# Gelu in front of the main loop: fewer VectorE steps, constants on ScalarE, multiplies on GpSimd, four PSUM banks for the running maxima

## The chip, the cores and the metric

The kernel runs on one core of one Trainium2 chip. The core has a matrix engine (TensorE, PE in the profile; its weight loads are PEld), VectorE (DVE), ScalarE (ACT), GpSimd (POOL) and SyncE (SP), which here only issues transfers. Each engine takes its own instructions strictly in the order in which the program wrote them, and waits where an operand isn't ready. The metric is the device time of one execution in microseconds; the median of three runs before the change is 1665.98 us (1665.54 to 1667.02).

## The reference

Two branches work on the same 2048 x 640 input and are mixed by a gate per token:

```python
def _A_ref(x, wq, wk, wv, wo):                  # H = 32 heads of 20, one shared k and v
    scores = jnp.einsum("bhqd,bkd->bhqk", q, k) * (Dh ** -0.5)
    p = _softmax(scores, axis=-1)
    o = jnp.einsum("bhqk,bkd->bhqd", p, v)
    return o.transpose(0, 2, 1, 3).reshape(B, S, H * Dh) @ wo
def _B_ref(x, w1, b1, w2, b2):                  # mixes over tokens: S = 2048, F = 1728
    h = _layernorm(x, axis=-1)
    u = _gelu(jnp.einsum("bsd,sf->bdf", h, w1) + b1)        # tanh form of gelu
    y = jnp.einsum("bdf,fs->bds", u, w2) + b2
    return y.transpose(0, 2, 1)
g = _sigmoid((x * gate_w).sum(-1, keepdims=True))
return g * _A_ref(...) + (1 - g) * _B_ref(...)
```

## The kernel before

Products that need more than the matrix engine's reduced precision are split in a high and a low part: a tile is rounded to `wh` (high), and `wl = raw - wh` is the low part; a product is then three matrix products (high by high, high by low, low by high).

The program has three stretches. First come projections of q, k and v and the layer norm (0 to about 96 us). Then follows the stretch that the change touches, called the **front loop** here (lines 565 to 601, about 96 to 168 us). Last comes the **main loop** (from line 1079 on), which does scores, exponentials, the product with v, the rest of the token mixing, and the output.

**The front loop** computes the first PRO = 8 of the 14 blocks of 128 columns of `h @ w1` for one half of the channels. A block is 16 *steps* (one row tile of 128 tokens each); a step is three products, each cut into two halves of 64 rows that go to two banks of PSUM, `pu0` and `pu1` (six matrix instructions a step, line 586). Four steps use one *chunk* of weights `wr`, `wh`, `wl`, so a block has four chunks, called hf 0 to hf 3. Ahead of each chunk `w1_upto` (line 118) prepares the chunk that is used three chunks later: the high part by ACT (line 126) for chunks below 4 * PRO = 32 and by POOL (line 128) from there on, the low part by POOL always (line 129), and it has SP fetch the raw weights of a further chunk (line 101). There are four buffers each of `wr`, `wh` and `wl`, so a chunk's high part can't be written before PE is through with the chunk four places earlier.

Between the steps stand 48 *leads* (`lead`, line 569): each issues two matrix instructions for the row maxima of the attention scores (line 479, tile `ms`) and two VectorE reductions that read them from PSUM (line 482, tile `mp`). They are spread from step 3 to step 122 of the 128. Before the change `ms` rotates through three banks, the pool `ps_m`; the pool `ps_g`, one bank, lies unused until the main loop; `pu0` and `pu1` have two banks each on the other side of PSUM.

After the last step of a block `gelu` (line 515) writes one ACT instruction, bias added while reading `pu0` (line 519; `id` in the text), and hangs the rest on the list `chain`. After each step of the next block `pop_chain` takes one entry, `None` for nothing. So entry *i* stands in each engine's queue behind step *i* of the next block, and `w1_upto` for hf 1, 2 and 3 stands in front of steps 4, 8 and 12. Before the change the entries are

```python
chain.extend((None, None, add, None, cube, tanh, None, prod_p, None, None, None, high, None, low))
```

| entry | what it writes | engine, line |
|---|---|---|
| 2 `add` | add the half in `pu1`; then square | DVE 525; ACT 522 |
| 4 `cube` | (square + constant) times x | DVE 529 |
| 5 `tanh` | tanh | ACT 532 |
| 7 `prod_p` | plus one; times x | POOL 545, 546 |
| 11 `high` | high part of the result | ACT 535 |
| 13 `low` | low part | POOL 538 |

For the last of the eight blocks `add` and the square are written at once, and the rest comes in the main loop by another list (`cube_p`, `tanh`, `prod_p`, `high_p`), where `settle` pops it. Between the two loops line 1016 prepares one more chunk.

**The main loop** puts its score and maximum products alternately into the banks of `ps_m` and `ps_s` (three each, `next_bank`, line 459), and token mixing products into `ps_g`. `ps_s` and `ps_o` open at lines 603 and 604 over the banks that `pu0` and `pu1` leave. The order of all queues is the program's own (`tc.manual_schedule`, line 170).

Of the kernel before, what the change touches and what calls it, by code (L numbers as in the profile page):

```python
# [9 lines left out]
F32 = mybir.dt.float32  # L10
F32R = mybir.dt.float32r
AF = mybir.ActivationFunctionType
ALU = mybir.AluOpType
AX = mybir.AxisListType
PSUM = bass.MemoryType.PSUM
DRAM = bass.MemoryType.DRAM

P = 128
# [6 lines left out]
NB = 512  # L25
# [3 lines left out]
PRO = 8  # L29
# [10 lines left out]
def mix_kernel(ctx: ExitStack, tc: tile.TileContext, A_x, A_wq, A_wk, A_wv, A_wo,  # L40
               B_x, B_w1, B_b1, B_w2, B_b2, gate_w, out):
    nc = tc.nc
# [3 lines left out]
    def f32(ap):  # L46
        return ap.bitcast(F32)
# [10 lines left out]
    bias = const.tile([P, 32], F32, name="bias")  # L58
# [19 lines left out]
    right = ExitStack()  # L78
# [13 lines left out]
    def w1_load(n):  # L92
        while len(w1raw) < min(n, len(chunks)):
            c = len(w1raw)
            wr = w1r.tile([P, HS, P], F32, name="wr")
            if c < W2:
                fc, hf = chunks[c]
                rows = slice(hf * HS * P, (hf + 1) * HS * P)
                for o in range(0, P, P if fc < FC - 1 else FT):
                    fw = P if fc < FC - 1 else FT  # L100
                    nc.sync.dma_start(out=wr[:, :, o:o + fw],
                                      in_=B_w1[rows, fc * P:fc * P + fw].rearrange("(c p) f -> p c f", p=P))
            else:
                st, hf = chunks[c]
                cols = slice(st * P, (st + 1) * P)
                nf = min(HS, FC - 1 - hf * HS)
                if hf == 3:
                    for h in range(2):
                        nc.sync.dma_start(out=wr[64 * (1 - h):64 * (2 - h), 2:, :],
                                          in_=B_w2[:2 * P, cols].rearrange("(c h p) s -> h p c s", c=2, h=2)[h])  # L110
                nc.sync.dma_start(out=wr[:, :nf, :],
                                  in_=B_w2[hf * HS * P:(hf * HS + nf) * P, cols].rearrange("(c p) s -> p c s", p=P))
                if nf < HS:
                    for o in range(0, P, FT):
                        nc.sync.dma_start(out=wr[o:o + FT, nf, :], in_=B_w2[(FC - 1) * P:, cols])
            w1raw[c] = wr

    def w1_upto(n):
        while fetched[0] < min(n, len(chunks)):
            c = fetched[0]  # L120
            w1_load(c + 1)
            wr = w1raw[c]
            wh = w1p.tile([P, HS, P], F32R, name="wh")
            wl = w1p.tile([P, HS, P], F32R, name="wl")
            if c < 4 * PRO:
                nc.scalar.activation(wh, wr, AF.Copy)
            else:
                nc.gpsimd.tensor_copy(wh, wr)  # L128
            nc.gpsimd.tensor_sub(wl, wr, f32(wh))  # L129
            w1t[c] = wh, wl  # L130
            fetched[0] += 1
            w1_load(c + 4)
# [22 lines left out]
    def new_q(n):  # L155
        if n < NU:
            qtiles[n] = load_q(n, "qst")
# [289 lines left out]
    u_lo = [view(t, UC * HD2, UC) for t in (u0, slot[0])]  # L447
    pp_pool = ctx.enter_context(tc.tile_pool(name="pp", bufs=11))
    ev = ctx.enter_context(tc.tile_pool(name="ev", bufs=1))
    ps_m = ctx.enter_context(tc.tile_pool(name="ps_m", bufs=3, space=PSUM))  # L450
    ps_g = ctx.enter_context(tc.tile_pool(name="ps_g", bufs=1, space=PSUM))
    mpool = ctx.enter_context(tc.tile_pool(name="mpool", bufs=2))
    mmpool = ctx.enter_context(tc.tile_pool(name="mmpool", bufs=2))

# [3 lines left out]

    def next_bank():
        if not ring:  # L460
            return ps_m.tile([P, NB], F32, name="ms")
        ring[0] ^= 1
        return ps_m.tile([P, NB], F32, name="ms") if ring[0] else ps_s.tile([P, NB], F32, name="s")
    given = [0, 0]
# [2 lines left out]
    def ms_next(b):  # L467
        k = given[b]
        if k >= 32 * NU:
            return None  # L470
        given[b] += 1
        n, r = divmod(k, 32)
        (kq, pr), qt = divmod(r // 4, 2), r % 4

        def step():
            if n not in mtiles:
                mtiles[n] = mpool.tile([P, 16, 4], F32, name="mp")
            ms = next_bank()
            nc.tensor.matmul(ms, qmax[n][64 * b:64 * b + 60, pr, qt * P:(qt + 1) * P],  # L479
                             kst[64 * b:64 * b + 60, kq * NB:(kq + 1) * NB], start=True, stop=True)  # L480
            c = (2 * b + pr) * 4 + qt
            nc.vector.tensor_reduce(mtiles[n][:, c, kq:kq + 1], ms, axis=AX.X, op=ALU.max)  # L482
            issued[b] += 1
            if min(issued) == 32 * n + 1:
                new_qmax(n + 1)

        return step
# [25 lines left out]
    chain = []  # L513

    def gelu(d, fc, accs):
        both = fin.tile([P, D], F32, name="yo")
        xg, t1 = both[:, :HD2], both[:, HD2:]
        hi, lo = u_hi[d][:, fc, :], u_lo[d][:, fc, :]
        nc.scalar.activation(xg, accs[0][:, :HD2], AF.Identity, bias=bias[:, NS + fc:NS + fc + 1])

        def square():
            nc.scalar.activation(t1, xg, AF.Square)

        def add():
            nc.vector.tensor_add(xg, xg, accs[1][:, :HD2])  # L525
            square()

        def cube():
            nc.vector.scalar_tensor_tensor(t1, t1, 1.0 / 0.044715, xg, op0=ALU.add, op1=ALU.mult)

        def tanh():
            nc.scalar.activation(t1, t1, AF.Tanh, scale=GC * 0.044715)

        def high():
            nc.scalar.activation(hi, t1, AF.Copy)

        def low():
            nc.gpsimd.tensor_sub(lo, t1, f32(hi))

        def cube_p():  # L540
            nc.gpsimd.tensor_scalar(t1, t1, 1.0, 1.0 / 0.044715, op0=ALU.mult, op1=ALU.add)
            nc.gpsimd.tensor_mul(t1, t1, xg)

        def prod_p():
            nc.gpsimd.tensor_scalar(t1, t1, 1.0, 1.0, op0=ALU.mult, op1=ALU.add)
            nc.gpsimd.tensor_mul(t1, t1, xg)

        def high_p():
            nc.gpsimd.tensor_copy(hi, t1)
            nc.gpsimd.tensor_sub(lo, t1, f32(hi))  # L550

        if len(accs) == 2 and fc == PRO - 1:
            add()
            chain.extend((cube_p, None, tanh, prod_p, high_p))
        elif len(accs) == 2:
            chain.extend((None, None, add, None, cube, tanh, None, prod_p, None, None, None, high, None, low))
        else:
            chain.extend((square, cube_p, None, tanh, prod_p, high_p))

# [2 lines left out]
        if f:  # L562
            f()

    with tc.tile_pool(name="psb", bufs=2, space=PSUM, side="right") as psb:
        at, skip, last = 0, 3, NS * PRO - 6
        one_by_one[0] = True

        def lead():
            for b in range(2):  # L570
                ms_next(b)()
            ms_done()

        for fc in range(PRO):
            pu = [psb.tile([P, NB], F32, name=f"pu{r}") for r in range(2)]
            for hf in range(4):
                w1_upto(4 * fc + hf + 4)
                for f in [q_parts_due.pop(0) for _ in range(min(len(q_parts_due), 1 + fc // 5))] if fc else []:
                    f()
                wh, wl = w1t.pop(4 * fc + hf)  # L580
                for c in range(HS):
                    st = hf * HS + c
                    for k, (w, h) in enumerate(((wh, h_hi[0]), (wh, h_lo[0]), (wl, h_hi[0]))):
                        for r in range(2):
                            rows = slice(64 * r, 64 * r + 64)
                            nc.tensor.matmul(pu[r][:, :HD2], w[rows, c, :], h[rows, st, :],  # L586
                                             start=(st == 0 and k == 0), stop=(st == NS - 1 and k == 2))
                    done = [max(0, min(x, last) - skip) * LEAD // (last - skip) for x in (at, at + 1)]
                    if done[1] > done[0]:
                        lead()  # L590
                    at += 1
                    pop_chain()
                if fc == 1 and hf == 0:
                    new_q(0)
                if fc == PRO - 2 and hf == 2:
                    assert not q_parts_due
                    one_by_one[0] = False
                    fetch_max(0)
            gelu(0, fc, pu)
            if fc == PRO - 3:  # L600
                store_max(0)

    ps_s = ctx.enter_context(tc.tile_pool(name="ps_s", bufs=3, space=PSUM))
    ps_o = ctx.enter_context(tc.tile_pool(name="ps_o", bufs=1, space=PSUM))

# [488 lines left out]
    for n in BLOCKS:  # L1094
# [3 lines left out]
        i = 0  # L1098
# [29 lines left out]
    for c in range(CUT // P, DC):  # L1128
        r = min(P, HEAD - c * P)
# [14 lines left out]
    for i in range(4):  # L1144
        st = NS - 4 + i
        for d in range(2):
# [7 lines left out]
            if (i, d) in ((0, 0), (1, 0), (2, 1), (3, 0), (3, 1)):  # L1154
                nc.vector.scalar_tensor_tensor(at[:, :HD2], acc[:, :HD2], g_col[:, st:st + 1], parts[st][:, sl],
                                               op0=ALU.mult, op1=ALU.add)
# [29 lines left out]
```

## Time and profile before

| | |
|---|---|
| median of three runs | 1665.98 us |
| the profiled execution | 1666.11 us, of which the span from first to last instruction is 1664.3 us |
| granted clock of TensorE over the span | 0.999 |
| front loop, first to last product of line 586 | 96.2 to 168 us |
| first product of the main loop (line 942) | 167.96 us |

A line of the profile names the engine, the line of the kernel, the operation, the tile written and the tiles read. In a timeline the first number is the start in us from the span's beginning and the second the time that the row covers; "x4" joins four instructions in a row; what stands in brackets is idle time of that engine just before, and what ended it. In a list of waits the numbers are the total, how often, and the longest.

### The profile page before, as it was taken

How to read it: one execution, taken by the hardware profiler on the slowest of the kernel's cores; microseconds unless marked ns; L12 is line 12 of the kernel's file. 1: busy time of each engine (PE TensorE's matmuls, PEld its weight loads, DVE VectorE, ACT ScalarE, POOL GpSimd, SP SyncE). 2: the span in 40 equal slices, each digit the busy share in tenths (PEclk: the TensorE clock that was granted, in tenths of full speed). 3: DMA queues.
4: the chain of work that ended last, by engine and by line, in shares of the span. 5: the costliest groups of instructions: out<-in, count | busy, mean ns of one | idle time of the engine just before them, and what ended most of it. 6: DMA issues, size and time to landing. Idle time of an engine off the chain costs nothing.

```text
span 1664.3 us, 38815 instructions
## 1 busy us (share of the span) xinstructions
PE 1655.7 (99%) x14865; PEld 1103.8 (66%) x14865; DVE 1434.6 (86%) x2732; ACT 1187.1 (71%) x2346; POOL 605.3 (36%) x759
## 2 busy tenths in 40 slices
PE   9999999999999999999999999999999999999998
PEld 7899666666666666666666666666666656666665
DVE  6689899989989999998998999989898998989933
ACT  4434777777777777777777777777777777777775
POOL 6578555455455554422232332122122220111210
PEclk9999999999999999999999999999999999999999
DMA  7665222322232222222222222212222121343611
GB/s 211 206 176 138 77 69 72 78 61 72 59 84 72 72 74 75 61 61 67 67 75 70 60 62 66 62 52 71 63 67 61 55 65 42 96 113 112 187 52 39
DMA packets 178304, 138.20 MB, mean 83 GB/s; under 512 B 33305, under 2 KB 144054, under 8 KB 178118
## 3 DMA queue, kind: packets, MB, share of 16 engines
q1 hardware_dynamic: 177830, 135.39, 29.3%
q8 instruction: 117, 1.92, 0.5%
q14 instruction: 69, 0.57, 0.1%
q10 hardware_dynamic: 288, 0.33, 0.1%
HBM read 102.36 MB, written 31.65 MB: 81 GB/s over the span
## 4 chain that ended last, share of the span: by engine, by line
PE 96%; issue 2%; DVE 1%; ACT 0%; POOL 0%; POOLq 0%; DVEq 0%; ACTq 0%
PE o L697 29%; PE ms L479 18%; PE s L663 13%; PE g L763 10%; PE g L942 7%; PE ms L663 5%; PE pp L298 4%; PE s L479 3%; PE pu L586 3%; PE g L888 2%; DVE mp L482 1%; PE ms L844 0%; PE pt L290 0%; PE pp L362 0%; ACT p L669 0%
## 5 line engine op out<-in xcount | busy, mean ns | idle before, releaser
L482 DVE TENSOR_REDUCE mp<-ms 128x1 f32<-128x512 f32 x1514 | 966.6, 686 | 126.2 <-PE ms L479 99.0
L669 ACT ACTIVATE p<-s 128x512 f32<-128x512 f32 x1512 | 822.4, 606 | 295.5 <-PE s L663 277.4
L479 PE MATMUL ms<-kst,qmx 60*128 60x512 f32 x1514 | 647.1, 434 | 1.7 <-DVE mp L482 1.7
L663 PE MATMUL s<-qst,kst 62*128 62x512 f32 x1512 | 600.5, 402 | 0.0
L697 PE MATMUL o<-p,v_sb 128*32 128x512 f32 x4096 | 511.3, 601 | 0.0
L479 PEld LDWEIGHTS ms<-kst,qmx 60*128 60x128 f32 x1514 | 279.0, 184 | 246.3 <-ACT p L669 104.2
L482 DVE TENSOR_REDUCE mp<-s 128x1 f32<-128x512 f32 x534 | 355.7, 684 | 12.0 <-PE s L479 11.7
L669 ACT ACTIVATE p<-ms 128x512 f32<-128x512 f32 x536 | 305.1, 600 | 56.5 <-PE ms L663 50.2
L663 PEld LDWEIGHTS s<-qst,kst 62*128 62x128 f32 x1512 | 278.6, 186 | 55.3 <-DVE flag L683 31.9
L942 PE MATMUL g<-slot,wh 64*128 64x320 f32 x1280 | 297.7, 312 | 0.0
L129 POOL TENSOR_TENSOR wl<-wr,wh 128x512 fp32r<-128x512 f32 x176 | 228.5, 1300 | 43.7 <-PE g L763 17.3
L479 PE MATMUL s<-kst,qmx 60*128 60x512 f32 x534 | 231.6, 443 | 0.4 <-DVE yo L525 0.4
L697 PEld LDWEIGHTS o<-p,v_sb 128*32 128x32 f32 x4096 | 97.5, 108 | 184.9 <-issue 176.9
L663 PE MATMUL ms<-qst,kst 62*128 62x512 f32 x536 | 216.8, 404 | 0.0
L942 PEld LDWEIGHTS g<-slot,wh 64*128 64x128 f32 x1280 | 211.8, 184 | 2.0 <-issue 1.7
L763 PE MATMUL g<-slot,wh 64*128 64x320 f32 x864 | 202.2, 313 | 0.0
L763 PE MATMUL g<-u,wh 64*128 64x320 f32 x864 | 201.8, 312 | 0.0
L942 PE MATMUL g<-slot,wl 64*128 64x320 f32 x640 | 199.8, 312 | 0.0
L719 POOL TENSOR_TENSOR ot<-ot,rl 128x512 f32<-128x512 f32 x30 | 31.5, 1051 | 346.2 <-DVE rl L718 346.2
L128 POOL CAST wh<-wr 128x512 fp32r<-128x512 f32 x144 | 88.1, 612 | 186.3 <-PE g L763 79.6
L763 PEld LDWEIGHTS g<-u,wh 64*128 64x128 f32 x864 | 143.5, 184 | 1.1 <-issue 1.1
L763 PEld LDWEIGHTS g<-slot,wh 64*128 64x128 f32 x864 | 143.6, 184 | 0.9 <-issue 0.8
(202 smaller groups left out, 2091.2 us busy)
## 6 DMA issues: line engine op xcount, KB each, us to landing
wr<-in_B_w_dram SPq DMA_DIRECT2D x152, 256.0 KB
qmx<-q_scr SPq DMA_DIRECT2D x192, 80.0 KB
qst<-q_scr SPq DMA_DIRECT2D x192, 80.0 KB
slot<-o_scr SPq DMA_DIRECT2D x20, 320.0 KB
y_scr<-yo SPq DMA_DIRECT2D x16, 320.0 KB
o_scr<-oh SPq DMA_DIRECT2D x124, 40.0 KB
o_scr<-ol SPq DMA_DIRECT2D x124, 40.0 KB
q_scr<-qh SPq DMA_DIRECT2D x19, 256.0 KB
```

Of the source, the lines that this page charges most:

```text
L128: nc.gpsimd.tensor_copy(wh, wr)
L129: nc.gpsimd.tensor_sub(wl, wr, f32(wh))
L298: nc.tensor.matmul(pp, w, t, start=first and n == 0, stop=not more and n == len(steps) - 1)
L479: nc.tensor.matmul(ms, qmax[n][64 * b:64 * b + 60, pr, qt * P:(qt + 1) * P], kst[64 * b:64 * b + 60, kq * NB:(kq + 1) * NB], start=True, s ...
L482: nc.vector.tensor_reduce(mtiles[n][:, c, kq:kq + 1], ms, axis=AX.X, op=ALU.max)
L586: nc.tensor.matmul(pu[r][:, :HD2], w[rows, c, :], h[rows, st, :], start=(st == 0 and k == 0), stop=(st == NS - 1 and k == 2))
L663: nc.tensor.matmul(s, kst[64 * b:64 * b + 62, kb * P:(kb + 1) * P], q[64 * b:64 * b + 62, pr, :], start=True, stop=True)
L669: nc.scalar.activation(p, s, AF.Exp, scale=SCALE)
L697: nc.tensor.matmul(o[32 * hh:32 * hh + 32, :], v_sb[:, kb, :], ptiles.pop((u, hh)), start=(kb == 0), stop=(kb == NS - 1), skip_group_check ...
L763: other_tile(half, nc.tensor.matmul(hold["p"][:, :HD2], w[r, fc % HS, :], u[d][r, fc, :], start=(hold["n"] == 1), stop=(hold["n"] == 6 * F ...
L888: other_tile(half, nc.tensor.matmul(hold["p"][:, :HD2], o[r, c, :], w[r, c, d * HD2:(d + 1) * HD2], start=(hold["n"] == 1), stop=(hold["n" ...
L942: other_tile(half, nc.tensor.matmul(hold["p"][:, :HD2], w[r, st % HS, :], h[d][r, st, :], start=(hold["n"] == 1), stop=(hold["n"] == 6 * NS)))
```

## The change

In the front loop and just behind it. `gelu`'s list for the first seven blocks loses VectorE's `cube`: ACT now adds the constant to the square in an instruction of its own (`plus`), POOL multiplies by x (`mul`), ACT adds the one after the tanh (`plus` again), and POOL multiplies once more, in place of its former add and multiply. Both `plus` stand directly behind the square and the tanh in ACT's queue. The entries move: the multiply at 4, tanh at 7 instead of 5, the second multiply at 9, `high` at 12 and `low` at 14. The limit for casts on ACT goes from chunk 32 to chunk 36, so chunks 32 to 35 are cast by ACT. PSUM is laid out anew: the pool `psl` has four banks for `ms`, `psb` has the four banks of `pu`, both are closed at the end of the front loop, and `ps_m` and `ps_g` open after it over the banks of `psl`.

```diff
@@ w1_upto
-            if c < 4 * PRO:
+            if c < 4 * PRO + 4:
                 nc.scalar.activation(wh, wr, AF.Copy)
             else:
                 nc.gpsimd.tensor_copy(wh, wr)
@@ mix_kernel
-    ps_m = ctx.enter_context(tc.tile_pool(name="ps_m", bufs=3, space=PSUM))
-    ps_g = ctx.enter_context(tc.tile_pool(name="ps_g", bufs=1, space=PSUM))
@@ next_bank
         if not ring:
-            return ps_m.tile([P, NB], F32, name="ms")
+            return psl.tile([P, NB], F32, name="ml")
@@ gelu
-        def cube():
-            nc.vector.scalar_tensor_tensor(t1, t1, 1.0 / 0.044715, xg, op0=ALU.add, op1=ALU.mult)
-
+        def plus(c):
+            nc.scalar.activation(t1, t1, AF.Copy, bias=c)
+
+        def mul():
+            nc.gpsimd.tensor_mul(t1, t1, xg)
+
+        def cubed():
+            add()
+            plus(1.0 / 0.044715)
+
+        def tanh_plus():
+            tanh()
+            plus(1.0)
...
-            chain.extend((None, None, add, None, cube, tanh, None, prod_p, None, None, None, high, None, low))
+            chain.extend((None, None, cubed, None, mul, None, None, tanh_plus, None, mul, None, None, high, None, low))
@@ the front loop
-    with tc.tile_pool(name="psb", bufs=2, space=PSUM, side="right") as psb:
+    with tc.tile_pool(name="psl", bufs=4, space=PSUM) as psl, \
+            tc.tile_pool(name="psb", bufs=1, space=PSUM) as psb:
...
+        first = [[psb.tile([P, NB], F32, name=f"pu{i}{r}") for i in range(2)] for r in range(2)]
         for fc in range(PRO):
-            pu = [psb.tile([P, NB], F32, name=f"pu{r}") for r in range(2)]
+            pu = [first[r][fc] if fc < 2 else psb.tile([P, NB], F32, name=f"pu{fc % 2}{r}") for r in range(2)]
...
+    ps_m = ctx.enter_context(tc.tile_pool(name="ps_m", bufs=3, space=PSUM))
+    ps_g = ctx.enter_context(tc.tile_pool(name="ps_g", bufs=1, space=PSUM))
     ps_s = ctx.enter_context(tc.tile_pool(name="ps_s", bufs=3, space=PSUM))
     ps_o = ctx.enter_context(tc.tile_pool(name="ps_o", bufs=1, space=PSUM))
```

## The prediction

> **What bounds the kernel now.** First the page's head, for what bounds the whole.
>
> ```profile
> span 1664.3 us, 38815 instructions
> PE 1655.7 (99%) x14865; PEld 1103.8 (66%) x14865; DVE 1434.6 (86%) x2732; ACT 1187.1 (71%) x2346; POOL 605.3 (36%) x759
> PE 96%; issue 2%; DVE 1%; ACT 0%; POOL 0%; POOLq 0%; DVEq 0%; ACTq 0%
> ```
>
> TensorE is busy for 99% of the span and holds 96% of the chain that ended last. So a delay in the front loop shifts everything behind it, unless the main loop can make it up; a gain there does the same. The share averages over stretches, so next come the busy times by window, for one block of the front loop and for a stretch of the main loop:
>
> ```profile
> core 0: us, PE busy (x) PEld busy (x) DVE busy (x) ACT busy (x) POOL busy (x), PEclk, DMA share, GB/s
> 149.30:158.30 9.00, 8.79 (x113) 8.51 (x112) 8.79 (x17) 4.02 (x8) 8.03 (x8) 1.00 0.64 160
> 300.00:600.00 300.00, 300.00 (x2770) 195.55 (x2767) 273.34 (x518) 230.28 (x458) 152.62 (x198) 1.00 0.28 73
> ```
>
> The block lasts 9.0 us, and VectorE is busy for 8.79 of them: here VectorE has next to no slack, POOL has one us, ACT is more than half idle. In the main loop (last row) TensorE has none. The list of waits over the front loop (96 to 168 us) agrees:
>
> ```profile
> PEld ms L479 <- DVE mp L482: 3.1, 5, 1.4
> PE ms L479 <- DVE mp L482: 1.7, 4, 1.1
> ```
>
> TensorE stands still for 3 to 5 us because a maximum bank hasn't been read. What a block would take without that, the chain of waits tells in its first part:
>
> ```profile
> 100.58 1.19 PE pu L586 x16
> ...
> 103.25 1.19 PE pu L586 x16
> ...
> 105.92 1.19 PE pu L586 x16
> ```
>
> The pattern of five steps with two leads repeats after 2.67 us, so 16 steps of pure TensorE work are 16/5 x 2.67 = 8.54 us.
>
> **The change part by part.** *Off VectorE:* `cube`. The groups by line (front loop) give its price, and the reductions':
>
> ```profile
> L482 DVE TENSOR_REDUCE mp<-ms 128x1 f32<-128x512 f32 x96 | 59.8, 684 | 2.8 <-PE ms L479 1.5 <-PE pu L586 0.7
> L529 DVE SCALAR_TENSOR_TENSOR yo<-yo 128x320 f32<-128x320 f32 x7 | 3.7, 522 | 0.5 <-ACT yo L522 0.5
> ```
>
> Back to back such an operation takes 0.39 to 0.40 us from start to start (107.09 to 107.49, quoted below), so VectorE is rid of seven times 0.40, 2.8 us. By itself that removes most of TensorE's standstill, and the fourth maximum bank gives TensorE one more product before it must wait.
>
> *The new queue order.* The price stands in one block's ACT and POOL timelines of before.
>
> ```profile
> 152.55 0.61 ACT L126 ACTIVATE wh<-wr 128x512 fp32r<-128x512 f32 x1
> 153.77 0.47 ACT L532 ACTIVATE yo<-yo 128x320 f32<-128x320 f32 x1 [0.61 <-DVE yo L529]
> 154.15 0.61 ACT L126 ACTIVATE wh<-wr 128x512 fp32r<-128x512 f32 x1
> 156.29 0.47 ACT L535 ACTIVATE u<-yo 128x320 fp32r<-128x320 f32 x1 [1.53 <-POOL yo L546]
> ```
>
> ```profile
> 153.24 1.64 POOL L129 TENSOR_TENSOR wl<-wr,wh 128x512 fp32r<-128x512 f32 x1 [0.88 <-ACT wh L126]
> 154.85 0.45 POOL L545 TENSOR_SCALAR yo<-yo 128x320 f32<-128x320 f32 x1
> 155.39 0.87 POOL L546 TENSOR_TENSOR yo<-yo 128x320 f32<-128x320 f32 x1
> 156.22 2.54 POOL L129 TENSOR_TENSOR wl<-wr,wh 128x512 fp32r<-128x512 f32 x2
> 158.72 0.88 POOL L538 TENSOR_TENSOR u<-yo,u 128x320 fp32r<-128x320 f32 x1
> 159.56 1.29 POOL L129 TENSOR_TENSOR wl<-wr,wh 128x512 fp32r<-128x512 f32 x1
> ```
>
> Read from these: a low part costs POOL 1.25 us from start to start (2.54 less 1.29), the multiply 0.83 (155.39 to 156.22), `low` 0.84. An ACT step of 320 columns frees ACT after 0.38 (153.77 to 154.15) and is done after 0.47; the cast is done after 0.61, and POOL starts its low part 0.08 later (152.55 + 0.61, then 153.24). From POOL back to ACT it is 0.03 (156.26 to 156.29). The low part of 1.64 ran while `cube` ran; without `cube` I take 1.29.
>
> Before, POOL goes without a gap from the low part of hf 1 over add and multiply to the low parts of hf 2 and hf 3 and to `low`: tanh waits for VectorE only, so the cast for hf 2 (154.15) is ready long before. After, tanh waits for POOL's multiply, which stands behind the low part of hf 1; behind tanh, in ACT's queue, stand `plus` and the cast for hf 2; and POOL's next instruction is the low part that needs this cast. So POOL is idle from the end of its first multiply until ACT has done three steps: 0.04 (multiply's end after its release of the queue) + 0.03 + 0.47 (tanh) + 0.03 + 0.38 (`plus`) + 0.61 (cast) + 0.08 = 1.64 us. The 0.03 between dependent ACT steps is seen where the main loop has such a pair:
>
> ```profile
> 192.93 0.55 ACT L519 ACTIVATE yo<-g,bias 128x320 f32<-128x320 f32 x1
> 193.51 0.47 ACT L522 ACTIVATE yo<-yo 128x320 f32<-128x320 f32 x1
> ```
>
> POOL's round is then 4 x 1.25 + 2 x 0.83 + 0.84 + 1.64 = 9.14 us a block, against TensorE's 8.54 and about 9.0 before. The add that it loses (0.54 from start to start) is included. And the round closes: `high` waits for the second multiply, the next block's `id` stands behind `high` in ACT's queue, VectorE's `add` waits for `id`, and behind `add` wait the reductions that free the maximum banks.
>
> *From where it counts.* The first chain runs in block 1:
>
> ```profile
> 104.53 0.53 ACT L519 ACTIVATE yo<-pu,bias 128x320 f32<-128x320 f32 x1 [1.37 <-POOL wl L129]
> 107.61 0.47 ACT L522 ACTIVATE yo<-yo 128x320 f32<-128x320 f32 x1 [2.03 <-DVE yo L525]
> 113.41 0.53 ACT L519 ACTIVATE yo<-pu,bias 128x320 f32<-128x320 f32 x1 [0.68 <-PE pu L586]
> 107.09 0.48 DVE L525 TENSOR_TENSOR yo<-yo,pu 128x320 f32<-128x320 f32 x1
> 107.49 1.28 DVE L482 TENSOR_REDUCE mp<-ms 128x1 f32<-128x512 f32 x2
> ```
>
> Up to the square at 107.61 nothing changes. Then `plus` 108.11, cast 108.49 to 109.10, low part 109.18, multiply 110.43 to 111.30, tanh 111.33, `plus` 111.83, cast 112.21 to 112.82, low part 112.90, multiply 114.15 to 115.02, `high` 115.05, and the second `id` at 115.43, where before it started at 113.41: 2.0 us late at once. Six rounds of 9.14 follow, and once the negation of the first maxima on POOL, 0.83 (143.34 to 144.17):
>
> ```profile
> 143.34 0.26 POOL L495 TENSOR_SCALAR mm<-mm 128x16 f32<-128x16 f32 x1 [0.92 <-DVE mm L493]
> 143.95 0.22 POOL L497 TENSOR_TENSOR mn<-mm,mn 128x16 fp32r<-128x16 f32 x1
> ```
>
> The eighth `id` starts at 115.43 + 54.84 + 0.8 = 171.1. TensorE itself, with four banks and a full round of weights ahead, ends its front products near 167.7 as before; what is late is `id`.
>
> *The hand-over*, before:
>
> ```profile
> 168.10 0.53 ACT L519 ACTIVATE yo<-pu,bias 128x320 f32<-128x320 f32 x1 [2.46 <-PE pu L586]
> 168.71 0.49 DVE L525 TENSOR_TENSOR yo<-yo,pu 128x320 f32<-128x320 f32 x1 [2.00 <-ACT yo L519]
> 169.12 0.68 DVE L482 TENSOR_REDUCE mp<-ms 128x1 f32<-128x512 f32 x1
> 169.26 0.50 PE L479 MATMUL s<-kst,qmx 60*128 60x512 f32 x1 [0.41 <-DVE yo L525]
> 170.32 0.60 ACT L669 ACTIVATE p<-ms 128x512 f32<-128x512 f32 x1 [0.62 <-PE s L479]
> ```
>
> After: `id` 171.1, `add` 171.7, the main loop's first reduction 172.1 (3.0 later than 169.12), square 172.2, the cast of chunk 35 that POOL did before, first exponential about 173.1 (2.8 later). TensorE may run ahead of both: in the new layout its second maximum bank is free, its fourth bank is one that `id` reads, so it gets some 2 us of mixing products done; but then it waits until VectorE and ACT have run through the same work, and the next mixing products wait for a VectorE flag behind the reductions. I count the whole 3.0. The casts that POOL loses lie beside other work: nothing. SP's fetch of the raw weights for four chunks on waits for POOL's low part, so it gets late with POOL; it is wanted a whole round later, and I count nothing. If it didn't land in time, the casts would start still later, which belongs to the last rival below.
>
> **Sum:** 1666.11 (the profiled execution; 1664.3 span and 1.8 around it) + 3.0 = 1669.1; the median of the runs is 0.13 lower, so **1669.0**.
>
> *Bounds.* No row shows ACT adding a constant without a function; the nearest below is a 16-wide step (0.20), above the `id` (0.53). With 0.27 less in seven rounds the end comes 1.9 earlier, with 0.06 more 0.4 later.
>
> ```profile
> 95.25 0.20 ACT L350 ACTIVATE ez<-z_col 128x16 f32<-128x16 f32 x1
> ```
>
> The path through `add` is the other danger. From the second multiply's end to the next block's low part of hf 1 it holds 0.03 + 0.38 (`high`), 0.53 + 0.08 (`id`), 0.49 + 0.03 (`add`), 0.47 + 0.03 (square), 0.38 (`plus`), 0.61 + 0.08 (cast): 3.11 us, while POOL has 3 instructions, 1.25 + 0.84 + 1.25 less 0.04, 3.30. It is 0.19 short of setting the round. If `add` must first wait out a reduction, 0.62 (59.8 over 96), the round grows by up to 0.43: 2.6 us in six. So this case spans 1667.1 to 1671.6. On the multiply, the Trainium skill ("GPSIMD Engine Reference", Engine selection) advises VectorE for elementwise work, GpSimd being about twice as slow with two inputs. The trace agrees (0.87 against 0.48); by twice 0.48, an estimate from that page, each round would be 0.18 longer and the end 1.3 us later.
>
> **The rivals.** *Faster: the round doesn't close.* If POOL, its low parts wanted only three chunks (6.4 us) later, catches up within each block, TensorE sets the pace: eighth `id` at 104.53 + 7 x 8.54 = 164.3, 3.8 earlier, less 0.4 for chunk 35's cast on ACT: 1662.7. For it speaks that VectorE is the one named in TensorE's waits; against it, that the steps from `id` to `id` wait for each other and sum to 9.14 less 0.19, 8.95 us, whatever POOL's reserve. The Trainium skill ("Perfetto Trace Analysis", Optimizing Scalar/DVE Operations) says that with a saturated VectorE, work may well go to Scalar or even GpSimd; the windows show that saturation, and this rival is what the rule would give.
>
> *No change:* `id` late, but the main loop's six banks and the products done ahead absorb it: 1666 to 1666.7. Against it: VectorE is busy 273 of 300 us there, and what TensorE did ahead is all it gains.
>
> *Slower still:* the growing lag reaches TensorE inside the front loop, which waits for low parts or for banks behind a blocked `add`. It decides once POOL is 4.4 us behind (6.4 less about 2 for cast and low part); with rounds of 9.5 the last `id` is 6 x 0.36, 2.2 us, later than my 171.1, and TensorE's own waits come on top: 5 to 7 us over before, 1672.
>
> **How the numbers follow.** Late `id` handed on 0.58, faster 0.20, absorbed 0.12, slower still 0.10. A measurement tells 0.2%, 3.3 us, from no change; the bound at 1669.3 cuts the likeliest case a little above its middle (0.25 above, 0.33 below). Slower 0.25 + 0.10 = 0.35; within 0.33 + 0.12 and a quarter of the faster case, 0.50; faster 0.15. The range goes from the faster case to the likeliest's upper bound, 1662.7 to 1671.6; the likeliest's own is 1667.1 to 1671.6.
>
> **What would show it.** After the change POOL's timeline should have a gap of about 1.6 us between the first multiply and the next low part, waiting for ACT's cast; ACT's `id` should come some 9.1 us apart, and late against the last product of its block; VectorE should wait for it in front of `add`, over 8 us in all; TensorE's waits for reductions should shrink. The first exponential should start near 173. It is wrong if `id` keeps within half a us of TensorE's block ends, or if the distance of the first exponential from before isn't found again at the end.

## The result, and the profile after

The changed kernel takes 1670.82 us (median of nine runs, 1669.87 to 1671.51); before, in nine runs, it was 1665.98. The ratio is 1.0027, 95% interval 1.0018 to 1.0037: slower by 4.8 us. The forecast was 1669.0 in a range from 1662.7 to 1671.6, with 0.35 for slower by over 0.2%, 0.50 for within.

The profiled execution took 1671.31. From its page:

```profile
span 1669.5 us, 38815 instructions
PE 1657.7 (99%) x14865; PEld 1106.2 (66%) x14865; DVE 1431.0 (86%) x2725; ACT 1195.6 (72%) x2364; POOL 603.2 (36%) x755
...
PE 96%; issue 3%; POOL 1%; DVE 0%; ACT 0%; POOLq 0%; DVEq 0%
```

The work moved as the diff says: VectorE has seven instructions less, ACT 18 more (14 constants, four casts), POOL four less (its casts), and the number in all is the same. Yet the span is 5.2 us longer. Nothing on this page says why; POOL with 1% on the chain that ended last is the first hint, for before it had none.

The waits of the front loop and the hand-over (96 to 172 us), the rows that matter:

```profile
ACT yo L527 <- POOL yo L547: 17.6, 7, 3.2
POOL wl L129 <- ACT wh L126: 15.6, 10, 2.4
ACT u L530 <- POOL yo L547: 12.0, 7, 1.8
...
PEld ml L477 <- DVE mp L480: 2.0, 4, 0.6
...
PE ml L477 <- DVE mp L480: 0.7, 2, 0.4
```

Line 527 is tanh, 547 POOL's multiply, 530 `high`, 477 and 480 the maxima. TensorE's waits for reductions fell from 3.1 and 1.7 to 2.0 and 0.7, which is what VectorE's relief and the fourth bank were expected to give. Before, the list had

```profile
POOL wl L129 <- ACT wh L126: 11.9, 10, 2.4
ACT u L535 <- POOL yo L546: 10.8, 7, 1.5
...
ACT yo L532 <- DVE yo L529: 4.5, 7, 0.8
```

(line 532 is tanh, 529 `cube`, 535 `high`). So tanh now waits 17.6 us for POOL in seven blocks, where it waited 4.5 for VectorE, and POOL's waits for ACT's casts have grown from 11.9 to 15.6. One block of both, as it repeats, in the timeline of POOL and then of ACT:

```profile
154.87 2.53 POOL L129 TENSOR_TENSOR wl<-wr,wh 128x512 fp32r<-128x512 f32 x2
157.36 0.88 POOL L547 TENSOR_TENSOR yo<-yo 128x320 f32<-128x320 f32 x1
159.84 1.29 POOL L129 TENSOR_TENSOR wl<-wr,wh 128x512 fp32r<-128x512 f32 x1 [1.60 <-ACT wh L126]
161.10 0.87 POOL L547 TENSOR_TENSOR yo<-yo 128x320 f32<-128x320 f32 x1
```

```profile
153.26 0.51 ACT L517 ACTIVATE yo<-pu,bias 128x320 f32<-128x320 f32 x1
153.66 0.62 ACT L126 ACTIVATE wh<-wr 128x512 fp32r<-128x512 f32 x1
154.32 0.47 ACT L520 ACTIVATE yo<-yo 128x320 f32<-128x320 f32 x1
...
158.27 0.47 ACT L527 ACTIVATE yo<-yo 128x320 f32<-128x320 f32 x1 [2.46 <-POOL yo L547]
158.77 0.47 ACT L544 ACTIVATE yo<-yo 128x320 f32<-128x320 f32 x1
159.15 1.14 ACT L126 ACTIVATE wh<-wr 128x512 fp32r<-128x512 f32 x2
...
162.37 0.51 ACT L517 ACTIVATE yo<-pu,bias 128x320 f32<-128x320 f32 x1
```

Here the reader sees the round: POOL's multiply ends at 158.24, tanh starts at 158.27, its constant at 158.77, the cast at 159.15, done at about 159.76, and POOL goes on at 159.84 after 1.60 us of idleness. The bias step `id` (line 517) comes at 153.26 and again at 162.37, 9.11 later. Over the whole front loop it starts at 104.91, 115.91, 125.05, 134.20, 143.30, 153.26, 162.37 and 171.49: distances of 11.0, 9.14, 9.15, 9.10, 9.96 (the block with the negation), 9.11 and 9.12.

At the hand-over, TensorE's timeline and then the busy times in windows:

```profile
172.63 0.79 PE L477 MATMUL s<-kst,qmx 60*128 60x512 f32 x1 [4.04 <-DVE yo L523]
172.63 0.63 PE L955 MATMUL g<-slot,wl 64*128 64x320 f32 x1
...
173.33 0.47 PE L955 MATMUL g<-slot,wh 64*128 64x320 f32 x1
173.60 0.47 PE L955 MATMUL g<-slot,wl 64*128 64x320 f32 x1
```

```profile
core 0: us, PE busy (x) PEld busy (x) DVE busy (x) ACT busy (x) POOL busy (x), PEclk, DMA share, GB/s
160.00:168.60 8.60, 8.59 (x107) 8.28 (x103) 6.74 (x12) 4.29 (x10) 7.40 (x7) 1.00 0.43 115
168.60:172.60 4.00, 0.00 (x0) 0.00 (x0) 0.51 (x2) 1.73 (x4) 3.60 (x4) 0.80 0.32 91
172.60:177.60 5.00, 4.97 (x27) 4.93 (x29) 2.71 (x5) 4.01 (x8) 3.13 (x4) 0.50 0.77 191
```

TensorE is through with the front loop at 167.8, does five mixing products and one maximum product, and then does nothing for 4.0 us, because the second maximum product waits for VectorE's `add` (line 523), which waits for `id`. And when it goes on, the granted clock is 0.50 over the next five microseconds: a mixing product takes 0.47 in place of 0.30, and they follow 0.27 apart (173.33, 173.60) where before it was 0.15. The same windows before show a clock of 1.00:

```profile
168.60:172.60 4.00, 3.59 (x33) 3.10 (x31) 3.43 (x7) 2.77 (x7) 3.75 (x6) 1.00 0.76 197
172.60:177.60 5.00, 5.00 (x44) 2.83 (x45) 3.35 (x7) 3.72 (x9) 3.78 (x5) 1.00 0.64 175
```

So the stall costs its length and then slow products behind it.

The chain of waits has the first product with v, the end of the hand-over, at 174.90 before and after at

```profile
179.71 1.85 PE o L710 x16
```

4.8 us later. From there to the end nothing changes: the second, hundredth and last of these groups are all 4.7 to 5.0 us later than before.

### The profile page after: what moved, and what is told of

It is laid out like the page before. It is cut to its first block, busy times and chain, and to the rows that moved or that the text cites. A ratio compares the mean times of both kernels' runs of the same rounds, so it can differ in the third digit from the quotient of the medians.

```text
span 1669.5 us, 38815 instructions
## 1 busy us (share of the span) xinstructions
PE 1657.7 (99%) x14865; PEld 1106.2 (66%) x14865; DVE 1431.0 (86%) x2725; ACT 1195.6 (72%) x2364; POOL 603.2 (36%) x755
## 4 chain that ended last, share of the span: by engine, by line
PE 96%; issue 3%; POOL 1%; DVE 0%; ACT 0%; POOLq 0%; DVEq 0%
PE o L710 29%; PE ms L477 18%; PE s L676 13%; PE g L776 10%; PE g L955 7%; PE ms L676 5%; PE pp L298 4%; PE s L477 3%; PE pu L597 2%; PE g L901 2%; PE ml L477 1%; PE pt L290 0%; PE pp L362 0%; PE ms L857 0%; POOL wl L129 0%
## 5 line engine op out<-in xcount | busy, mean ns | idle before, releaser
L480 DVE TENSOR_REDUCE mp<-ms 128x1 f32<-128x512 f32 x1418 | 906.4, 685 | 123.8 <-PE ms L477 98.5
L477 PE MATMUL ms<-kst,qmx 60*128 60x512 f32 x1418 | 616.2, 436 | 0.0
L477 PEld LDWEIGHTS ms<-kst,qmx 60*128 60x128 f32 x1418 | 262.2, 185 | 242.1 <-ACT p L682 104.2
```

## The experiments

Each kernel was timed beside the kernel before on the same chip (24 or 25 runs of it in each of two sets: 1666.27 and 1666.07). As the kernel before differs by up to 0.3 us between the sets (1665.98 beside the change), comparisons across sets are in doubt by as much. The theory is that POOL and ACT close a round of waits; rival one is that the work added to ACT and POOL costs by its amount, rival two that the new PSUM layout costs.

**The same instructions, tanh one entry later.**

```diff
-chain.extend((None, None, cubed, None, mul, None, None, tanh_plus, None, mul, None, None, high, None, low))
+chain.extend((None, None, cubed, None, mul, None, None, None, tanh_plus, None, mul, None, high, None, low))
```

> The changed kernel with tanh and its constant one entry later, at 8, behind ACT's cast for hf 2, and the second multiply at 10; not one instruction more or less. Theory (closed round): POOL's idle 1.6 us between the first multiply and the next low part go, the eighth bias step starts near 165.7 instead of 171.5, TensorE neither idles at the hand-over nor is gated down, and the time is 1663.8 (before less 2.2). Rival one (the added ACT and POOL work itself costs): the same work, so 1670 to 1671. Rival two (the new PSUM layout costs): unchanged layout, so 1670 to 1671.

Measured: 1665.01 us (1663.99 to 1665.24, 11 runs), ratio to before 0.9990 (0.9981 to 0.9999). Against the change that is 5.8 us for two moved entries, so rivals one and two fall as the main cause: work and layout are those of the change. Its POOL timeline, one block:

```profile
152.10 1.29 POOL L129 TENSOR_TENSOR wl<-wr,wh 128x512 fp32r<-128x512 f32 x1 [0.22 <-ACT wh L126]
153.35 0.88 POOL L547 TENSOR_TENSOR yo<-yo 128x320 f32<-128x320 f32 x1
154.19 1.29 POOL L129 TENSOR_TENSOR wl<-wr,wh 128x512 fp32r<-128x512 f32 x1
155.44 0.87 POOL L547 TENSOR_TENSOR yo<-yo 128x320 f32<-128x320 f32 x1
```

The gap is gone: the multiply at 153.35 is followed by the low part at 154.19, for its cast no longer stands behind tanh. The eighth `id` came at 165.93 (expected 165.7), but the time is 1.2 above what was expected. At the hand-over TensorE still waits 2.0 us for `add` (list of waits). The profile is of one of five runs that took 1663.99 to 1664.44 us at a granted clock of 0.999 to 1.000; the other six took 1665.01 to 1665.24 at 0.998 or 0.999. The clock may have been halved in those six, which would be much of the 1.2; no trace of one shows it.

**The list of before with the new layout and casts.**

```diff
+        def cube():
+            nc.vector.scalar_tensor_tensor(t1, t1, 1.0 / 0.044715, xg, op0=ALU.add, op1=ALU.mult)
...
-chain.extend((None, None, cubed, None, mul, None, None, tanh_plus, None, mul, None, None, high, None, low))
+chain.extend((None, None, add, None, cube, tanh, None, prod_p, None, None, None, high, None, low))
```

> The list of before (VectorE's cube, POOL's add and multiply) with the new PSUM layout and the four more casts on ACT. Theory: the layout is a gain by itself, TensorE's waits for reductions shrink from some 4.8 us to about 1, the eighth bias step starts near 165.3, and the time is 1663.4. Rival two (layout): as slow as the change, 1669 or more. Rival one (added work): 1666 or below, so this run parts rival two from the others.

Measured: 1663.40 us (1662.84 to 1664.65, 11 runs), ratio 0.9982 (0.9974 to 0.9991). Rival two falls: the layout is the part of the change that gains, 2.9 us (the four casts alone change nothing, as the last run shows). The list of waits shows by what, 3.1 us of TensorE's waits for reductions having become

```profile
PEld ml L477 <- DVE mp L480: 0.8, 2, 0.4
```

**The change's list and casts with the old layout** (three maximum banks, pools as before).

```diff
-            if c < 4 * PRO:
+            if c < 4 * PRO + 4:
...
-chain.extend((None, None, add, None, cube, tanh, None, prod_p, None, None, None, high, None, low))
+chain.extend((None, None, cubed, None, mul, None, None, tanh_plus, None, mul, None, None, high, None, low))
```

> The change's list and casts with the PSUM layout of before (three maximum banks). Theory: the round closes all the same, bias steps 9.1 us apart, the eighth near 171.5, TensorE idles 3 to 4 us in front of the main loop and runs at half clock behind it: 1670 to 1671.5. Rival two (layout): 1663 to 1666. If three banks make TensorE wait so much that POOL gets time back, it is less than 1670, but not under 1667.

Measured: 1671.52 us (1670.34 to 1672.77, 8 runs), ratio 1.0030 (1.0020 to 1.0041). As slow as the change. Once the round sets the pace, a bank more or less decides nothing: the 2.9 us of the layout are lost in it. TensorE stands still for 3.33 us at the hand-over here, and its waits for reductions are 3.6 and 2.5 us, no less than before the change, although VectorE has no `cube` to do.

**One more instruction in the round.**

```diff
 def tanh_plus():
     tanh()
     plus(1.0)
+    plus(0.0)
```

> The changed kernel with one more ACT instruction behind tanh and its constant, adding 0.0: seven instructions of 0.47 us on an engine that is idle for half of the front loop. Theory: it lies in the closed round, so each round grows by 0.41 (0.03 and 0.38), bias steps come 9.54 us apart, the eighth near 174.3 (2.9 later), and the time is 1673.5 to 1674.2. Rival: ACT's reserve hides it, 1670.8.

Measured: 1674.69 us (1674.24 to 1675.9, 5 runs), ratio 1.0051 (1.0039 to 1.0064), 3.9 us over the change. Seven instructions of 0.47 us on an engine that is idle for half of this stretch cost 3.9 us (3.6 when each kernel is set against the kernel before of its own set): they aren't hidden. The ACT timeline shows two `id` steps

```profile
155.71 0.51 ACT L517 ACTIVATE yo<-pu,bias 128x320 f32<-128x320 f32 x1
...
161.22 0.98 ACT L544 ACTIVATE yo<-yo 128x320 f32<-128x320 f32 x2
...
165.33 0.51 ACT L517 ACTIVATE yo<-pu,bias 128x320 f32<-128x320 f32 x1
```

9.62 apart instead of 9.11. The round grew by 0.50, not the 0.41 expected: the constant before must now be finished (0.47 + 0.03) before the next one starts, where the cast behind it, which doesn't need it, started after 0.38.

**The idle time at the hand-over filled with useless products** (18 of 128 x 512, results never read).

```diff
+    for i in range(3):
+        fill = ps_m.tile([P, NB], F32, name="ms")
+        for j in range(6):
+            nc.tensor.matmul(fill, kst[:, :P], kst[:, :NB], start=True, stop=True)
     ring.append(0)
```

> The changed kernel with 18 useless products of 128 x 512 between the front loop and the main loop, some 3.9 us of TensorE time, into banks of ps_m that nobody reads before they are overwritten. Theory (the idle 4.0 us let the granted clock fall to 0.50, which then costs some 1.4 us): TensorE stays busy, the clock stays at 1.00 behind the hand-over, the mixing products come 0.147 us apart instead of 0.267, and the time falls in spite of more work, to 1669.3. Rival (the products behind the hand-over are slow because of the transfers at that time, 0.77 of the DMA engines): they stay slow, and the time is 1670.8 or more, by up to 3.9 if the added products reach beyond the wait.

Measured: 1670.26 us (1670.04 to 1671.24, 8 runs), ratio 1.0026 (1.0015 to 1.0036); the change, run again in the same set: 1671.00 (1669.94 to 1671.29, 6 runs), ratio 1.0030 (1.0017 to 1.0042).

> The changed kernel once more, beside the run with the idle time filled: 1670 to 1671.5.

The medians differ by 0.7 the way that was expected, by half the amount, and the intervals overlap. The granted clock over the run is 0.999 or 1.000 in all eight runs of the filled kernel, and 0.998 in five of the six of the change. The profiles show where. TensorE and the busy times of the filled kernel:

```profile
167.07 4.38 PE L1095 MATMUL ms<-kst 128*128 128x512 f32 x18
171.39 0.50 PE L477 MATMUL ms<-kst,qmx 60*128 60x512 f32 x1
...
172.60:177.60 5.00, 5.00 (x44) 4.10 (x41) 3.87 (x8) 4.74 (x11) 3.50 (x5) 1.00 0.87 211
```

and the same window of the change run again:

```profile
172.60:177.60 5.00, 5.00 (x35) 4.96 (x35) 2.88 (x6) 4.02 (x9) 2.61 (x3) 0.60 0.85 212
```

With the DMA engines as busy (0.87 and 0.85), the clock stays at 1.00 and 44 products are done instead of 35. So it was the idle time, not the transfers. In these two profiles the front loop starts within 0.03 us and the eighth `id` within 0.02; the first product with v comes at 177.69 when filled and at 178.69 when idle. The half clock cost 1.0 us there.

**Another order of the change's list.**

```diff
-chain.extend((None, None, cubed, None, mul, None, None, tanh_plus, None, mul, None, None, high, None, low))
+chain.extend((None, None, cubed, mul, None, tanh_plus, None, mul, None, None, None, high, None, low))
```

> The changed kernel with its list in another order: first multiply at 3, in front of the low part of hf 1, tanh and its constant at 5, second multiply at 7, high at 11, low at 13. Theory: POOL multiplies while ACT casts for hf 1, ACT does tanh while POOL makes that low part, so no engine waits for a round; VectorE has neither cube nor a late bias step to wait for, TensorE sets the pace, the eighth bias step starts near 164.5, and the time is 1662.6, the least of all. If some other cost of the change remains hidden (the multiply on POOL, the constants on ACT), it stays above the 1663.4 of the list of before with the new layout.

Measured: 1662.97 us (1662.27 to 1663.43, 11 runs), ratio 0.9982 (0.9973 to 0.9991). This beats both kernels. POOL's timeline:

```profile
151.31 0.88 POOL L547 TENSOR_TENSOR yo<-yo 128x320 f32<-128x320 f32 x1 [0.22 <-ACT yo L544]
152.15 1.29 POOL L129 TENSOR_TENSOR wl<-wr,wh 128x512 fp32r<-128x512 f32 x1
153.40 0.87 POOL L547 TENSOR_TENSOR yo<-yo 128x320 f32<-128x320 f32 x1
154.24 2.53 POOL L129 TENSOR_TENSOR wl<-wr,wh 128x512 fp32r<-128x512 f32 x2
```

The multiply now stands in front of the low part of hf 1, so ACT does tanh while POOL makes that low part, and the long waits are gone: in this block tanh waits 0.47 us for POOL, and POOL 0.22 for ACT. The eighth `id` came at 164.42 (expected 164.5). Against the list of before with the new layout its ratio is the same, 0.9982; that it is the least of all can't be told from these runs, so taking `cube` off VectorE has no shown gain once there are four banks.

**The casts alone, on the kernel before.**

```diff
-            if c < 4 * PRO:
+            if c < 4 * PRO + 4:
```

> The kernel before with only the limit for casts on ACT moved from chunk 32 to chunk 36. Theory: POOL's casts lie beside other work, and the chunk cast in front of the exponentials costs ACT 0.5 us that waits anyway: 1666.0 to 1666.6, no change. Rival: the casts are the costly part of the change, 1667 or more.

Measured: 1666.29 us (1665.62 to 1667.65, 11 runs), ratio 1.0001 (0.9993 to 1.0010). No change.

**All profiles side by side.** Three starts from the timelines, in us: the first product of the front loop, the eighth `id`, and the first product with v.

| kernel | first product | eighth `id` | first with v | first to `id` | `id` to v |
|---|---|---|---|---|---|
| before | 96.17 | 168.10 | 174.82 | 71.93 | 6.72 |
| change | 96.58 | 171.49 | 179.64 | 74.91 | 8.15 |
| change, again | 95.84 | 170.80 | 178.69 | 74.96 | 7.89 |
| idle filled | 95.87 | 170.82 | 177.69 | 74.95 | 6.87 |
| old layout | 96.78 | 171.85 | 180.36 | 75.07 | 8.51 |
| one more constant | 96.55 | 174.93 | 183.25 | 78.38 | 8.32 |
| tanh later | 96.40 | 165.93 | 172.65 | 69.53 | 6.72 |
| list of before, new layout | 95.87 | 164.75 | 171.48 | 68.88 | 6.73 |
| multiply first | 96.13 | 164.42 | 171.14 | 68.29 | 6.72 |
| casts only | 96.00 | 167.61 | 174.35 | 71.61 | 6.74 |

From `id` to the first product with v it is 6.72 to 6.74 us in every kernel whose TensorE stands still for at most 2.0 us there, and 7.9 to 8.5 in the four where it stands still for 3.3 to 4.5; filled, it is 6.87. The first column moves by up to 0.9 between executions, also between two of the same kernel.

## Why the prediction was right, and where it wasn't

*The bound.* That TensorE has no reserve in the main loop, so that a delay at its start is found again at the end, held: 4.8 us at the first product with v, 4.9 at the last. The first exponential came at 174.40, not near 173: 4.1 us later than before, with the clock still at 0.50.

*VectorE's relief and the fourth bank.* TensorE's waits for reductions shrink, as was said, and with another order of the list the gain arrives in the time. But the layout with the fourth bank brings it nearly alone (0.8 us of waits in place of 3.1). That taking `cube` off VectorE would by itself remove most of the standstill isn't borne out: with three banks the waits were 3.6 and 2.5 us, though there the closed round holds back the reductions too, and with four banks the last 0.8 go from the list of waits, but no gain in the time can be told.

*The closed round.* Forecast: 1.64 us of idleness on POOL, a round of 9.14, the second `id` 2.0 late, the eighth at 171.1. Measured: 1.60, 9.10 to 9.15, the second `id` 2.1 later when counted from the first (11.00 against 8.88), and from the first product on the eighth `id` is 74.91 - 71.93 = 2.98 later; 171.49 is that plus a front loop that began 0.41 later in this execution. That the round is the cause, and not the amount of work, is shown from three sides: opened without touching an instruction (5.8 us faster than the change), lengthened by 0.50 a block (3.9 us slower), and with the banks of before (no better). The 1.29 us taken for a low part that no longer runs beside `cube` was right too. The faster rival described what happens when the round is open, and two kernels went there: 1663.0 and, with the list of before, 1663.4, against its 1662.7.

*The bounds.* The constant's price was open, by 1.9 us down and 0.4 up; it is that of the other ACT steps, 0.47 us. The path through `add` was the larger bound, 2.6 us up, and it didn't lengthen the round, which kept to 9.10 to 9.15.

*VectorE waits for `id`:* "over 8 us in all" was about right (8.0), but its place was not foreseen: 5.0 of it stand at the hand-over,

```profile
172.09 0.49 DVE L523 TENSOR_TENSOR yo<-yo,pu 128x320 f32<-128x320 f32 x1 [5.03 <-ACT yo L517]
```

and within the front loop TensorE's waits stayed below those of before.

*The hand-over is the step that failed in size.* The prediction counted "the whole 3.0" and let TensorE get "some 2 us of mixing products done" on a free second bank. Two things were wrong in it. The second maximum product didn't start on that bank; it waited for `add` as it did before the change (whether for its own bank or for the whole pool wasn't tried). That cost nothing by itself, since the whole 3.0 was counted, but TensorE had nothing to do for 4.0 us, where the prediction's own figures leave about 2.4 (front products done near 167.7, 2 us of mixing products, the next reduction at 172.1). And the half clock that came with the stall was missing from the sum altogether: 8.15 - 6.72 = 1.43 us in the first profile, 1.17 in the second, 0.15 when the time was filled. The first product with v, 4.82 us later than before, splits into 2.98 in the front loop, 1.43 behind `id`, and 0.41 of an earlier stretch that varies; that the 1.43 is the clock's rests on the filled run. The same sum without the 0.41 is 4.4, and the medians differ by 4.8; the remaining 0.4 wasn't pursued.

*The number.* 1670.82 lies within the range, 1.8 us over the forecast, but the outcome that came had been given 0.35 and the one within 0.2% had 0.50. The range reached up to 1671.6 because a longer round was allowed for. The round didn't get longer; what took up that room was the half clock, which the prediction doesn't name. That the range held the time is luck to this extent.

## What to carry to other kernels

When work moves between engines, count the queues before the instructions: an instruction that waits for another engine holds back everything behind it on its own, and if the other engine's next work is among that, the two take turns, however idle both look in the busy shares. Walk one period from release to release and compare its length with the pace of the bound engine; the cure may be a place in the order rather than less work. And a stall of the matrix engine can cost more than its length, as the one of 4.0 us did here.

## What the runs showed of the hardware

The price of the idle time was not expected. In the change TensorE stands still from 168.6 to 172.6; windows of 0.1 us show its granted clock at 0.50 from 171.0, still within the stall, to 177.8. In all four profiles with a stall of 3.3 to 4.5 us the half clock lasts 6.8 us, and it begins 1.8 to 3.3 us into the stall. What varies is how much of it is left when the products start again: 4.6 us (the change again), 5.2 (the change), 5.6 (one more constant) and 6.0 (old layout). The stretch from `id` to the first product with v is longer than before by 1.17, 1.43, 1.60 and 1.79 us, in the same order. In the kernel before, whose longest wait in this stretch was 1.1 us, the clock stayed at 1.00, and so it did in the profile of tanh later, with a wait of 2.0.

The rule is on a page of the Trainium skill ("TensorE: Matmul & The Clock Gate", What's actually happening): the clock is halved after an idle window of about 3.4 us and comes back after a busy window of about the same length, the window running freely. The traces agree with the halving, and the 6.8 us are twice that window. They differ in how long the stall must be: the clock fell 1.8 us after the last product in one profile, and a stall of 3.33 us was enough in another. By its own 2.4 us the prediction had no stall of the page's length; the term was lost with the bank that it took for free.

On tiles of 128 x 320 a dependent ACT step starts 0.50 us after the one that it needs (158.27, 158.77), an independent one 0.38 after (158.77, 159.15). In a chain of short steps on one engine that difference is part of every round.
